# Unit 1's prefix products taken from the scan of all units, in a Mamba-2 SSD kernel with a SiLU MLP behind it

## The chip, the cores and the metric

The kernel runs on one core of one Trainium2 chip. The time is the device time of one execution in microseconds (us). A core has a matrix engine (PE), a vector engine (DVE), a scalar engine (ACT), GpSimd (POOL) and SyncE (SP), whose queue here issues most of the DMA transfers. Each engine runs its own instruction queue in order, and waits on semaphores for the others.

## The reference

Inputs are x (4, 8, 768, 32), a (4, 8, 768), B and C (4, 8, 768, 16) in single precision, and two weights, (256, 2048) and (2048, 256), in double precision. The first block is a chunked state-space scan, the second an MLP on its output.

```python
log_a = np.log(np.clip(a, 1e-06, 1.0))
for c in range(nc):                       # chunks along the sequence
    cum = np.cumsum(la, axis=-1)
    M = einsum('bhin,bhjn->bhij', Cc, Bc) * exp(cum_i - cum_j) * causal
    y = M @ xc + (Cc @ state) * exp(cum)[..., None]
    state = exp(sum(la)) * state + sum_j(B_j x_j * exp(cum[-1] - cum_j))
x = attn_out.transpose(0, 2, 1, 3).reshape(B * S, H * D)      # (3072, 256)
h = x @ w_in
return (h * (1 / (1 + exp(-h)))) @ w_out                      # (3072, 256)
```

## The kernel before

The sequence is cut into 12 **units** of 256 rows, three for each batch, and a unit into chunks of 64. A unit u goes through these steps; the names are those of the schedule's tokens.

- **Loads**: `Ln` (B or C with rows on partitions), `Lt` (B or C in a layout for a 32x32 transpose), `Lx` (x), `lw` (a weight tile of 512 KB, in the double's two words).
- **Prefix products** of a inside a chunk, which replace the exponential of a cumulative sum: a scan along the free axis that multiplies, and restarts at each chunk because a zero stands at its first place and a one is added there. They are kept in `PFX[u]`, spread over 16 partitions for each head.
- **E**: the decay between two positions, a scan (L512) over a diagonal. For units 0 and 1 its input is made on the chip (`ia`, `A`, `AT`, `AU`, `as`, `ab`: load, clip, transpose, copy, copies, four transposes on PE). For later units `La` loads it from a DRAM buffer `az`.
- **B** scales B by E's last column (POOL, L520). **T** transposes C and B on DVE (L525), **tp/tq** on PE and ACT. **ce** masks C for the even and odd heads (ACT, with `par`, which `cP` makes). **g0** is C times B (PE, L585), **M** multiplies it with E (DVE, L600). **D** or **gd** is B times x (PE, L571), **S** the running state (DVE, L615), **SM** its masked copy (ACT), **C** is C times the prefix (L551, DVE or POOL), and **Y** the unit's output on PE (L635, L644).
- **The MLP**: units 0 and 1 use single-precision matmuls (`s`, L697, first layer; `n1`, L761, second layer). Later pairs of units split numbers in three parts (`xh`, `x`, `h`, `l`, `e`) and use `a`, `d` (L800) and `q` (L782). Each weight tile is first turned from doubles into singles: `u`, `v` on ACT (L294, L297), `w` on DVE (L303, L307, L310), `W` on POOL (L318), and then split by `H`, `lD`, `dD` and others.
- **z** is a warm-up matmul on zeros (L441).

**Two ways to a prefix.** Units 0 and 1 have their own: `ip` loads the unit's 256 values of a for all heads, each repeated on 16 partitions (L379); `P01` clips them (L475) and scans (L479). All other units read theirs from a DRAM buffer `ac`: `ir` loads a as 48 chunks by 8 heads in four parts (L383); `AA` clips it on POOL (L462), once for `az` and once for the scan; `AP` scans all chunks of all units in one DVE instruction over 48 partitions by 520 (L486); `AD` stores the result, `AD,4` to `az` (L468) and `AD,0` to `AD,3` one batch each to `ac` (L470); `Lp,u` loads a unit's part of `ac`, spread over 16 partitions, on SP (L237). `ca` and `co` are the memsets for the zeros and ones of that scan.

**The order** is written out by hand in `SCHEDULE`, a string of tokens that are carried out one after the other: each engine's queue holds its instructions in the order of the tokens, and `SLOTS` names the buffer that each tile takes. In the old order the steps for `ac` come late: `ir` is spread over the places after unit 1's Y, `AP` ran at 39.5 us, and unit 1's own prefix stands between the transposes and the first MLP matmul:

```text
u,5 w,5,0 ip,1,0 z,1 P01,1,0 tp,1 tq,1 s,0,0 ce,1,1 ce,1,0 g0,1 Lx,1,1,0 Lx,1,0,0 W,4 xh,0 w,5,1 si,0,0 B,1,0 P01,1,1 D,1
```

Of the kernel before, what the change touches and what calls it, by code (L numbers as in the profile page):

```python
# [28 lines left out]
Wd,12 x,0,1 lw,14 u,14 n1,11,0 n1,9,1 x,1,1 W,8 Ln,2,1,0,0 v,14 w,14,2 ir,0 si,1,0 n1,1,0 n1,1,1 H,0 n1,0,1 H,1 lw,6 v,6
w,6,2 n1,11,1 n1,10,1 ir,2 ir,1 u,6 lw,10 Wl,12 AA,0 AA,1 AD,4 w,6,0 AP w,6,1 AD,0 lw,2 Ln,2,0,0,0 ax,0,7 w,15,0 u,10  # L30
u,2 W,6 n1,8,0 AD,1 v,2 H,6 v,10 w,2,0 s,1,1 si,1,1 lw,3 tp,2 dD,7 v,3 v,15 u,3 w,2,1 w,2,2 W,2,0 Lt,3,1,3,0 lD,6 dD,6
w,14,0 n1,8,1 w,3,2 a,0,6 ax,0,6 w,15,2 W,2,1 s,1,2 si,1,2 H,2 d,0,7 w,14,1 dg,0,7 AD,2 w,3,0 w,15,1 d,0,6 dg,0,6 W,14
Lt,3,1,0,0 w,10,2 s,0,2 lw,9 u,9 v,9 Lt,3,1,2,0 Lt,3,1,1,0 T,3,1 H,4 si,0,2 n1,10,0 Lx,2,0,0 n1,12,1 La,2,0,0 w,3,1 tq,2
La,2,1,0 E,2,1 E,2,0 lD,4 w,9,0 W,15 n1,15,1 Lt,3,0,0,0 n1,12,0 B,2 ce,2,0 ce,2,1 Lt,3,0,3,0 g0,2 lw,11 u,11 Lp,2,0 C,2
M,2,1 Lx,2,1,0 gd,2 b,2,0 b,2,1 S,2,0 S,2,1 H,15 S,2,2 W,3 Lp,3,0 Lt,4,1,1,0 H,13 La,3,1,0 w,10,0 v,11 Lt,4,1,0,0
n1,15,0 SM,2,0 Wl,15 SM,2,1 w,10,1 W,10 ce,3,1 Lt,4,1,3,0 M,2,0 La,3,0,0 E,3,1 E,3,0 s,0,3 si,0,3 Lt,3,0,2,0 ce,3,0
n1,13,0 Lt,3,0,1,0 T,3,0 Y,2 Lx,3,1,0 Ln,3,0,0,0 y,2,0 y,2,1 xh,2 x,2,0 n1,5,0 x,2,1 Ln,3,0,1,0 s,1,3 w,9,1 g0,3 C,3 B,3
M,3,1 Lx,3,0,0 gd,3 b,3,0 b,3,1 S,3,0 S,3,1 Lt,4,0,1,0 w,9,2 n1,0,0 n1,14,1 Lx,4,0,0 Lt,4,0,0,0 La,4,0,0 S,3,2 W,9
n1,13,1 SM,3,0 M,3,0 SM,3,1 lD,0 Y,3 n1,2,1 n1,3,0 Lt,4,0,3,0 dD,0 La,4,1,0 w,11,0 w,11,1 y,3,0 y,3,1 xh,3 x,3,0 w,11,2
n1,2,0 W,11 H,10 a,1,0 Wl,10 Wm,10 n1,3,1 n1,4,0 Lt,4,1,2,0 T,4,1 x,3,1 si,1,3 S,3,3 Lp,4,0 C,4 ce,4,1 E,4,0 H,11 ax,1,0  # L40
d,1,0 E,4,1 ce,4,0 Lt,4,0,2,0 n1,5,1 Wl,11 Lx,5,1,0 Wl,13 dg,1,0 n1,4,1 T,4,0 H,8 lD,1 Ln,4,0,0,0 g0,4 lD,2 Ln,4,0,1,0
B,4 H,9 M,4,1 La,5,1,0 Wm,11 Lx,4,1,0 Wm,12 gd,4 b,4,0 lD,8 b,4,1 dD,1 n1,6,1 h,1,0 S,4,0 S,4,1 Lx,5,0,0 H,3 S,4,2
SM,4,1 n1,14,0 n1,6,0 SM,4,0 Lt,5,1,3,0 M,4,0 n1,7,0 Vn,0 Y,4 y,4,1 y,4,0 xh,4 l,1,0 n1,7,1 S,4,3 a,1,2 Vn,1 lD,9 dD,8
dD,2 H,5 a,1,1 ax,1,2 e,1,0 q,1,0,1,0 d,1,2 dD,9 q,1,0,0,1 Ln,5,0,0,0 ax,1,1 d,1,1 Wd,13 Lt,5,1,1,0 q,1,0,0,0 q,1,0,1,1
AD,3 Lt,5,1,0,0 dD,4 dg,1,2 Lt,5,0,3,0 h,1,2 a,1,4 dg,1,1 h,1,1 Lt,5,1,2,0 T,5,1 ce,5,0 Lt,5,0,2,0 ce,5,1 Lt,5,0,0,0
lD,3 a,1,3 Lp,6,0 dD,10 o,0,1,2 We,12 dD,3 x,4,1 x,4,0 l,1,2 e,1,2 ax,1,4 d,1,4 H,14 q,1,2,0,1 Ln,5,0,1,0 ax,1,3 d,1,3
l,1,1 La,5,0,0 E,5,0 dg,1,4 e,1,1 q,1,1,1,1 dg,1,3 Lt,5,0,1,0 h,1,3 q,1,1,0,1 E,5,1 T,5,0 g0,5 B,5 M,5,1 Lp,5,0 C,5 gd,5
b,5,1 lD,5 Lt,6,1,0,0 b,5,0 S,5,0 Lt,6,1,3,0 S,5,1 Wm,13 We,13 dD,5 q,1,2,1,1 La,6,0,0 q,1,2,0,0 a,1,5 Lx,6,1,0 Wl,14
# [840 lines left out]
```

## Time and profile before

| | us |
|---|---|
| median of three runs | 329.66 |
| lowest, highest | 329.29, 333.11 |
| the profiled execution | 329.1 |
| its span from the first to the last instruction | 327.4 |
| PE busy | 320.3 (98%) |
| DVE busy | 240.4 (73%) |
| ACT busy | 209.5 (64%) |
| POOL busy | 56.0 (17%) |
| granted clock, mean | 0.999 |

A row of the profile names the line of the kernel, the engine, the operation, what it writes and reads by tile names, and sizes as partitions by elements. In the timelines a row begins with its start from the span's start and its duration, and ends with the idle time of its engine before it and what ended that. Durations of neighbours on one engine overlap by some hundredths, so that the distance between starts is a little shorter than the duration.

### The profile page before, as it was taken

To read this page: it belongs to the slowest core of one execution; us is meant where nothing else is said; L and a number is where in the kernel's file an instruction comes from. 1 tells how busy PE (TensorE), PEld (TensorE's weight loads), DVE (VectorE), ACT (ScalarE), POOL (GpSimd) and SP (SyncE) were. 2 spreads that over 40 slices of the span, in tenths; PEclk is the share of its full clock that TensorE was granted. 3 is DMA by queue.
4 is the path that set the end of the run, shared out by engine and by line. 5 is a ranking of instruction groups with operands and counts; after the bars stand their busy time and mean duration, and the time that the engine had idled before them with its cause. 6 is when DMAs were issued, how large, how long until landed. Compare 5 with 4: busy or idle time off the path is not lost.

```text
span 327.4 us, 7519 instructions
## 1 busy us (share of the span) xinstructions
PE 320.3 (98%) x3064; PEld 243.4 (74%) x3067; DVE 240.4 (73%) x331; ACT 209.5 (64%) x319; POOL 56.0 (17%) x74
## 2 busy tenths in 40 slices
PE   8999999999999999999999999999999999999994
PEld 3478576655687777878887778878887788888883
DVE  4998999999988965877687299665787544635553
ACT  4679978648696846583771875837775455574641
POOL 1364766326102330001200010010001000000000
PEclk9999999999999999999999999999999999999999
DMA  6979966479872663423633306514042000050003
GB/s 162 206 200 272 296 175 192 51 148 135 148 127 46 105 115 53 86 36 64 147 74 70 44 1 117 104 26 96 3 74 37 7 2 2 0 88 0 2 1 64
DMA packets 94962, 29.27 MB, mean 89 GB/s; under 512 B 80000, under 2 KB 86912, under 8 KB 94928
## 3 DMA queue, kind: packets, MB, share of 16 engines
q1 hardware_dynamic: 90960, 25.71, 37.5%
q0 software_dynamic: 1616, 2.82, 5.1%
q10 hardware_dynamic: 2352, 0.26, 0.6%
q8 instruction: 24, 0.39, 0.5%
q14 instruction: 10, 0.08, 0.1%
HBM read 22.81 MB, written 3.34 MB: 80 GB/s over the span
## 4 chain that ended last, share of the span: by engine, by line
PE 94%; SPq 2%; DMA 1%; DVE 1%; issue 1%; DVEq 0%
PE hp L782 29%; PE ga L800 18%; PE gb L800 18%; PE hp L761 9%; PE hp L697 6%; PE o_ps L782 6%; PE ga L635 2%; PE ga L585 2%; PE ga L644 2%; DMA s2k<-in_C_dram 1%; PE gb L644 1%; PE ga L571 1%; SPq L262 0%; SPq L375 0%; PE o_ps L531 0%
## 5 line engine op out<-in xcount | busy, mean ns | idle before, releaser
L782 PE MATMUL hp<-r4k,s2k 128*128 128x512 f32 x400 | 110.0, 394 | 0.0
L651 DVE SCALAR_TENSOR_TENSOR r4k<-r4k,r4k 128x1024 fp32r<-128x1024 f32 (+1 forms) x42 | 50.5, 1202 | 51.3 <-ACT r4k L827 48.2
L782 PEld LDWEIGHTS hp<-r4k,s2k 128*128 128x128 f32 x400 | 74.0, 188 | 16.4 <-issue 0.3
L800 PE MATMUL ga<-raw,s2k 128*128 128x512 f32 x240 | 62.3, 395 | 0.0
L800 PE MATMUL gb<-raw,s2k 128*128 128x512 f32 x240 | 61.1, 390 | 0.0
L800 PEld LDWEIGHTS ga<-raw,s2k 128*128 128x128 f32 x240 | 44.7, 188 | 11.4 <-ACT ga L811 0.9
L800 PEld LDWEIGHTS gb<-raw,s2k 128*128 128x128 f32 x240 | 44.8, 188 | 9.9 <-ACT gb L811 0.5
L837 DVE SCALAR_TENSOR_TENSOR r4k<-r4k,r4k 128x1024 fp32r<-128x1024 f32 x40 | 49.2, 1231 | 3.4 <-DVE r4k L651 0.9
L827 ACT ACTIVATE r4k<-r4k 128x1024 fp32r<-128x1024 f32 x40 | 42.2, 1058 | 3.2 <-issue 1.3
L811 ACT ACTIVATE ga<-ga 128x1024 f32<-128x1024 f32 x21 | 21.1, 1007 | 24.6 <-PE ga L800 23.8
L811 ACT ACTIVATE gb<-gb 128x1024 f32<-128x1024 f32 x21 | 21.2, 1009 | 17.6 <-PE gb L800 13.3
L782 PE MATMUL o_ps<-r4k,s2k 128*128 128x512 f32 x80 | 30.7, 390 | 0.0
L761 PE MATMUL hp<-r4k,s2k 128*128 128x512 f32 x64 | 30.0, 602 | 0.0
L821 ACT ACTIVATE r4k<-gb 128x1024 f32<-128x1024 f32 x21 | 21.4, 1021 | 12.4 <-PE gb L800 9.9
L520 POOL TENSOR_TENSOR BT<-bn,ab 128x256 f32<-128x256 f32 x10 | 6.7, 672 | 129.5 <-DVE ab L512 123.3
L318 POOL TENSOR_TENSOR s2k<-s2k,s2k 128x512 uint32<-128x512 uint32 (+1 forms) x19 | 23.6, 1250 | 26.4 <-DVE s2k L307 13.7
L821 ACT ACTIVATE r4k<-ga 128x1024 f32<-128x1024 f32 x21 | 21.5, 1023 | 8.4 <-PE ga L800 8.2
L512 DVE TENSOR_TENSOR_SCAN ab<-ab,diag 128x512 f32<-128x512 f32 x20 | 24.8, 1265 | 0.0
L697 PE MATMUL hp<-r4k,s2k 128*128 128x256 f32 x96 | 22.3, 382 | 0.2 <-issue 0.2
L697 PEld LDWEIGHTS hp<-r4k,s2k 128*128 128x128 f32 x96 | 18.0, 190 | 4.0 <-issue 1.4
L761 PEld LDWEIGHTS hp<-r4k,s2k 128*128 128x128 f32 x64 | 11.6, 189 | 10.5 <-issue 9.6
L782 PEld LDWEIGHTS o_ps<-r4k,s2k 128*128 128x128 f32 x80 | 15.0, 188 | 3.2
(123 smaller groups left out, 384.8 us busy)
## 6 DMA issues: line engine op xcount, KB each, us to landing
ab<-az SPq DMA_DIRECT2D x20, 256.0 KB, 4.2
raw<-in_moe_w_in_dram SPq DMA_DIRECT2D x8, 512.0 KB, 4.2
raw<-in_moe_w_out_dram SPq DMA_DIRECT2D x8, 512.0 KB, 8.0
...
xt<-in_x_dram SPq DMA_DIRECT2D x20, 128.0 KB, 4.2
...
```

Of the source, the lines that this page charges most:

```text
L318: nc.gpsimd.tensor_tensor(out=u[:, :, fs], in0=u[:, :, fs], in1=v[:, :, fs], op=ALU.add)
L512: nc.vector.tensor_tensor_scan(out=o, data0=src, data1=diag.rearrange("p h t -> p (h t)"), initial=0.0, op0=ALU.mult, op1=ALU.add)
L644: nc.tensor.matmul(out=y[w][32 * q:32 * q + 32, c, 64 * k:64 * k + 64], lhsT=xc[64 * c:64 * c + 64, k, h], rhs=m[64 * c:64 * c + 64, k, h] ...
L651: nc.vector.scalar_tensor_tensor(out=l, in0=f32(h), scalar=BACK, in1=y, op0=ALU.mult, op1=ALU.add)
L697: nc.tensor.matmul(out=hp[:, i], lhsT=WT[j][:, kc, 128 * i:128 * i + 128], rhs=XM()[:, 2 * kc:2 * kc + 2, u], start=(kc == 0), stop=(kc == ...
L761: nc.tensor.matmul(out=NP[m], lhsT=WT[8 + f // 2][:, f % 2, 128 * m:128 * m + 128], rhs=GT[0, f // 2][:, f % 2], start=(n == 1), stop=(n = ...
L782: nc.tensor.matmul(out=ACC[P, c], lhsT=WK[8 + i, p][:, k, 128 * m:128 * m + 128], rhs={"h": HT, "l": LT, "d": DT}[p][P, i][:, k], start=(n ...
L800: nc.tensor.matmul(out=o, lhsT=WK[j, q][:, kc, 128 * i:128 * i + 128], rhs=xs[:, 2 * kc:2 * kc + 2], start=(start and q == "h" and kc == 0 ...
L811: nc.scalar.activation(t, t, AF.Copy, scale=1.0 + Z)
L821: nc.scalar.activation(g, t, AF.Silu, scale=BACK)
L827: nc.scalar.activation(t, GT[G, i], AF.Copy, scale=-LESS * Z)
L837: nc.vector.scalar_tensor_tensor(out=DT[G, i], in0=f32(HT[G, i]), scalar=-1.0, in1=f32(LT[G, i]), op0=ALU.mult, op1=ALU.subtract)
```

## The change

Unit 1 no longer makes a prefix of its own. `ip,1`, `P01,1,0` and `P01,1,1` leave the schedule (one load, one clip and one scan, with a memset), and `Lp,1` comes in: unit 1 reads its part of `ac` as the later units do. The steps that fill `ac` for batch 0 (`ir`, `ca`, `AA`, `co`, `AP`, `AD,0`) move ahead of unit 0's first matmuls on x. All other tokens are the same in kind and number, among them all loads, matmuls and warm-up matmuls, and stand in a new order from the first to the last; the buffer lists are new to match.

```diff
     def c_p01():
-        for u in range(2):
-            nc.vector.memset(pz01(u)[:, :, 0:1], 0.0)
+        nc.vector.memset(pz01(0)[:, :, 0:1], 0.0)
         nc.vector.memset(one01(), 0.0)
         nc.vector.memset(one01()[:, :, 0:1], 1.0)
...
 SCHEDULE = """
-Ln,0,0,0,1 ia,1 ci z,1 z,1 z,1 z,1 z,1 z,1 ia,0 Ln,0,0,1,1 cI z,1 ch cP ct ip,0,0 z,1 z,1 z,1 c1 cd A AT cp AU lw,0 z,1
-z,1 as,0,0 ab,0,0 P01,0,0 P01,0,1 as,0,1 ab,0,1 as,1,1 ab,1,1 E,0,0 u,0 z,1 z,1 z,1 Lt,0,1,3,0 v,0 w,0,0 w,0,2 w,0,1
-lw,4 W,0,1 z,1 B,0,0 z,1 z,1 v,4 Lt,0,1,1,0 u,4 z,1 z,1 Ln,1,1,1,0 z,1 E,0,1 B,0,1 z,1 z,1 z,1 Lt,0,1,0,0 Lt,0,1,2,0
-T,0,1 as,1,0 z,1 z,1 z,1 tp,0 tq,0 E,1,1 Lx,0,0,0 Lx,0,1,0 D,0 S,0,0 z,1 w,4,2 z,1 S,0,1 z,1 w,4,0 S,0,2 ce,0,0 ce,0,1
-g0,0 M,0,1 lw,7 v,7 Ln,1,0,0,0 SM,0,0 M,0,0 z,1 z,1 SM,0,1 u,7 w,4,1 w,7,0 z,1 z,1 w,7,2 w,7,1 lw,5 v,5 w,5,2 W,0,0
-S,0,3 Ln,1,1,0,0 ab,1,0 E,1,0 C,0 Y,0 X0,0,1 Ln,1,0,1,0 B,1,1 X0,0,0 u,5 w,5,0 ip,1,0 z,1 P01,1,0 tp,1 tq,1 s,0,0 ce,1,1
-ce,1,0 g0,1 Lx,1,1,0 Lx,1,0,0 W,4 xh,0 w,5,1 si,0,0 B,1,0 P01,1,1 D,1 s,0,4 M,1,1 lw,1 u,1 lw,12 S,1,0 W,5 v,1 ca S,1,1
...
+Ln,0,0,1,1 cI ci z,1 ch z,1 z,1 z,1 z,1 z,1 z,1 c1 z,1 Ln,0,0,0,1 cd ia,1 ir,0 z,1 ct z,1 ia,0 A z,1 Lt,0,1,0,0 AT AU
+as,0,1 Lx,0,1,0 as,0,0 z,1 cp ir,2 ip,0,0 P01,0,0 P01,0,1 z,1 ab,0,1 E,0,1 as,1,1 ab,1,1 tp,0 tq,0 ca ir,1 ab,0,0 z,1
+z,1 ir,3 AA,0 E,0,0 lw,4 Lt,0,1,3,0 u,4 B,0,1 z,1 z,1 Lt,0,1,1,0 z,1 z,1 Lt,0,1,2,0 T,0,1 cP z,1 ce,0,1 z,1 z,1 v,4 AA,1
+co AP z,1 ce,0,0 z,1 w,4,0 E,1,1 w,4,2 lw,0 z,1 z,1 z,1 Ln,1,0,1,0 z,1 Lx,0,0,0 z,1 AD,0 B,0,0 g0,0 M,0,1 Ln,1,0,0,0 z,1
+D,0 as,1,0 S,0,0 S,0,1 z,1 u,0 v,0 w,0,0 z,1 S,0,2 SM,0,1 M,0,0 w,0,1 w,0,2 ab,1,0 z,1 E,1,0 B,1,1 z,1 Ln,1,1,0,0 lw,5
+SM,0,0 u,5 S,0,3 w,5,0 C,0 v,5 w,4,1 Y,0 X0,0,0 X0,0,1 xh,0 z,1 Ln,1,1,1,0 tp,1 ce,1,1 W,0,0 w,5,2 W,0,1 s,0,0 lw,7
+ce,1,0 Lp,1,0 tq,1 C,1 B,1,0 w,5,1 g0,1 M,1,1 Lx,1,1,0 Lx,1,0,0 D,1 S,1,0 u,7 si,0,0 S,1,1 S,1,2 lw,1 SM,1,1 v,1 u,1
+lw,8 SM,1,0 W,4 w,7,0 S,1,3 s,0,4 M,1,0 Lt,3,1,1,0 w,1,2 v,7 v,8 W,5 s,0,5 w,1,0 w,1,1 W,1,1 u,8 w,8,0 w,7,2 si,0,5 lw,6
...
```

Three new helper functions (`w_copy`, `f_ds`, `f_dl`) are defined, and no token of the schedule calls them.

More of the change, by code (lines that the diff above doesn't have):

```diff
@@ L29 @@
[L29 to L48, printed above, removed]
@@ new lines @@
+lD,4 Ln,5,0,1,0 n1,5,0 n1,3,1 M,4,0 n1,7,0 Vn,0 Y,4 y,4,1 l,1,0 n1,2,1 lD,8 lD,2 dD,2 y,4,0 La,5,0,0 lD,9 dD,8
+Lt,5,1,3,0 xh,4 dD,5 Lt,5,1,1,0 Lt,5,1,2,0 T,5,1 e,1,0 dD,1 Wl,15 Wm,15 Lt,5,0,3,0 a,1,2 ax,1,2 Vn,1 o,0,1,2 ce,5,1
+Lt,5,0,0,0 a,1,1 ax,1,1 d,1,2 dg,1,2 q,1,0,1,0 Lt,5,0,1,0 dD,9 q,1,0,0,0 Wd,15 h,1,2 x,4,1 Wd,12 O,0,1,2,1,0 d,1,1
+Lt,5,0,2,0 AD,3 We,13 ce,5,0 q,1,0,1,1 dg,1,1 h,1,1 q,1,0,0,1 Wm,12 dD,4 S,4,3 a,1,4 ax,1,4 a,1,3 l,1,2 e,1,2 dD,10
+q,1,2,1,1 Lx,5,0,0 ax,1,3 La,5,1,0 d,1,4 dg,1,4 Lp,5,0 d,1,3 dg,1,3 h,1,3 q,1,2,0,1 l,1,1 e,1,1 q,1,1,1,0 E,5,0 E,5,1
@@ L100 @@
+O,5,0,2,2,0 Va,5,1 qd,5,7,0,1 qd,5,6,0,1 qd,5,7,1,1 Vt,5,1,0 Vt,5,1,1 ot,5,1,0 Vt,5,1,3 Vt,5,1,2 ot,5,1,1 or,5,1,0
+os,5,1,0,0 or,5,1,1 os,5,1,1,1
 """
@@ L335, in w_part, with w_copy @@
         nc.scalar.activation(t, f32(WK[n, "h"]), AF.Copy, scale=1.0 if p == "l" else Z)
+    def w_copy(n):
+        t = WK[n, "l"] = small(f"l{n}", [128, 2, WF], FR)
+        nc.sync.dma_start(out=f32(t).rearrange("p k f -> p (k f)"), in_=f32(WK[n, "h"]).rearrange("p k f -> p (k f)"))
     def w_more(n, p):
@@ L755, with f_ds, f_dl @@
     NP = {}
+    def f_ds(i):
+        spill[i] = dram.tile([128, 1024], FP32, name=f"spill{i}")
+        nc.sync.dma_start(out=spill[i], in_=GT[0, i].rearrange("p k n -> p (k n)"))
+    def f_dl(i):
+        g = GT[0, i] = large(f"R0_{i}", [128, 2, 512])
+        nc.sync.dma_start(out=g.rearrange("p k n -> p (k n)"), in_=spill[i])
+    spill = {}
     def f_n(f, m):
```

136 lines of the change are left out of this document (74 added, 62 removed), and 6 rows, old and new, of the table SLOTS.

## The prediction

> **What bounds the kernel now.** I read the page's first part and its stage table first, since they say which engine is full and where it is not.
>
> ```profile
> span 327.4 us, 7519 instructions
> PE 320.3 (98%) x3064; PEld 243.4 (74%) x3067; DVE 240.4 (73%) x331; ACT 209.5 (64%) x319; POOL 56.0 (17%) x74
> ...
> 0.00:10.00 10.00, 8.45 (x34) 3.95 (x35) 5.71 (x21) 3.78 (x6) 1.41 (x10) 1.00 0.73 163
> 10.00:20.00 10.00, 9.21 (x191) 5.87 (x199) 9.57 (x19) 7.95 (x19) 5.18 (x8) 1.00 0.88 185
> 20.00:30.00 10.00, 9.72 (x193) 8.15 (x193) 8.76 (x20) 7.54 (x16) 5.49 (x9) 1.00 0.97 289
> 30.00:40.00 10.00, 10.00 (x37) 6.62 (x36) 9.52 (x12) 9.16 (x17) 6.84 (x7) 1.00 0.90 264
> ```
>
> The columns of a stage are its length, then busy time of PE, PEld, DVE, ACT and POOL, then the granted clock, the DMA share and GB/s. From 30 us on to the tail PE is busy for all of every stage, so the time is set by when PE's dense stretch begins, by PE's own work after that, and by the tail. The change cannot shorten PE's work (its list has the same matmuls, the 36 warm-up ones included), so I look for the step that opens the dense stretch, in the chain of waits and in PE's timeline:
>
> ```profile
> 6.36 4.75 DMA s2k<-in_C_dram
> 14.38 1.21 DVE ab L600 x2
> 15.73 0.27 PE ga L635 x2
> ...
> 1.27 4.45 PE L441 MATMUL o_ps<-s2k 128*128 128x512 bf16 x10 [1.27 <-DVE s2k L388]
> 8.07 3.40 PE L441 MATMUL o_ps<-s2k 128*128 128x512 bf16 x15
> 17.25 0.83 PE L531 MATMUL o_ps<-ident,s2k 128*128 128x128 f32 x4 [0.16 <-issue]
> 17.94 1.99 PE L697 MATMUL hp<-r4k,s2k 128*128 128x256 f32 x8
> ```
>
> Unit 0's output Y (L635) starts at 15.73, when VectorE (DVE) has finished M (L600); its transposes (L531) and then the first MLP matmul (L697, at 17.94) follow. Before 17.94 PE mostly runs warm-up matmuls. The last long wait on that path is the C load, landing at 11.11; after it DVE works without a break.
>
> **The head, step by step.** In the new order unit 0's head has more ahead of it, and I walk the two queues that matter. These are DVE's and ACT's rows; a cost below is the distance from one start to the next where DVE runs without a break.
>
> ```profile
> 2.32 0.22 DVE L422 TENSOR_REDUCE par<-hm 128x1 f32<-128x4 f32 x2 [0.97 <-POOL hm L417]
> 4.10 0.22 DVE L448 TENSOR_SCALAR s2k<-s2k 32x128 f32<-32x128 f32 x1 [0.41 <-DMA s2k<-in_a_dram]
> 4.46 0.28 DVE L410 MEMSET s2k<- 128x260 f32 x1
> 6.22 0.43 DVE L495 COPY s2k<-s2k 128x512 f32<-128x512 f32 x1
> 6.56 0.29 DVE L475 TENSOR_SCALAR s2k<-s2k 128x256 f32<-128x256 f32 x1
> 6.88 0.70 DVE L479 TENSOR_TENSOR_SCAN s2k<-s2k,s2k 128x260 f32<-128x260 f32 x1
> 7.50 1.20 DVE L512 TENSOR_TENSOR_SCAN ab<-hp,diag 128x512 f32<-128x512 f32 x1
> 8.61 0.40 DVE L303 TENSOR_SCALAR s2k<-s2k 128x512 f32<-128x512 f32 x1
> 8.93 0.69 DVE L310 SCALAR_TENSOR_TENSOR s2k<-raw,s2k 128x512 uint32<-128x512 uint32 x1
> ...
> 11.30 0.65 DVE L525 STREAM_TRANSPOSE ct<-s2k 128x256 f32<-128x256 f32 x1 [0.21 <-DMA s2k<-in_C_dram]
> 11.79 1.17 DVE L512 TENSOR_TENSOR_SCAN ab<-hp,diag 128x512 f32<-128x512 f32 x1
> ...
> 14.11 0.28 DVE L615 SCALAR_TENSOR_TENSOR st<-st,s2k,hp 128x64 f32<-128x64 f32 x1
> 14.30 0.69 DVE L600 TENSOR_TENSOR ab<-gb,ab 128x512 f32<-128x512 f32 x1
> ...
> 36.99 1.09 DVE L310 SCALAR_TENSOR_TENSOR s2k<-raw,s2k 128x512 uint32<-128x512 uint32 x1
> 39.51 1.23 DVE L486 TENSOR_TENSOR_SCAN r4k<-r4k,r4k 48x520 f32<-48x520 f32 x1
> ```
>
> And the loads and GpSimd (POOL) steps, as SP's and POOL's timelines and the list of DMA issues show them:
>
> ```profile
> 0.81 1.64 SPq L375 DMA_DIRECT2D s2k<-in_a_dram  x2
> 2.50 0.63 SPq L379 DMA_DIRECT2D s2k<-in_a_dram  x1
> 20.73 0.45 SPq L383 DMA_DIRECT2D s2k<-in_a_dram  x1
> ...
> 10.04 0.73 POOL L318 TENSOR_TENSOR s2k<-s2k,s2k 128x256 uint32<-128x256 uint32 x1 [6.81 <-DVE s2k L307]
> 10.73 0.85 POOL L520 TENSOR_TENSOR BT<-s2k,ab 128x128 f32<-128x128 f32 x2
> 26.63 0.52 POOL L425 MEMSET r4k<- 48x520 f32 x1
> 36.61 0.93 POOL L462 TENSOR_SCALAR s2k<-s2k 48x512 f32<-48x512 f32 x1
> 37.78 0.77 POOL L462 TENSOR_SCALAR r4k<-s2k 48x512 f32<-48x512 f32 x1
> 41.05 0.63 POOL L470 DMA_DIRECT2D ac<-r4k  x1 [1.68 <-DVE s2k L307]
> ...
> xt<-in_x_dram SPq DMA_DIRECT2D x20, 128.0 KB, 4.2
> ac<-r4k POOLq DMA_DIRECT2D x4, 24.4 KB, 4.0
> az<-s2k POOLq DMA_DIRECT2D x1, 96.0 KB, 6.0
> ```
>
> *SP.* One of the four chunk loads (ir, L383, 0.45 us of SP each) now stands between the two ia loads, so the second ia is issued 0.5 us later and the clip (4.10) comes at 4.6. That costs nothing by itself: the transpose of a (AT) stands behind warm-up matmuls on PE, 11 of them instead of 10, at 0.445 us each, so it starts near 6.2 instead of 5.7, and the copies after it 0.45 us later. The load ip for unit 0's prefix is now seventh on SP: 0.81 + 1.64 for the ia pair, two ir, a C load and an x load at about 0.45 each, with gaps of 0.05, gives an issue at 4.5 instead of 2.50. Before, its user (L475) ran at 6.56 without a wait for it, so it landed within 4.06 us of its issue; the ia load took 2.35 (issued at 1.75, used at 4.10). So it lands between 6.85 and 8.55, and I take the middle, 7.7.
>
> *DVE up to the first scan.* The copy (6.67), its 0.34 and the three memsets (about 0.45 together, moved behind it) end at 7.45. The prefix then waits for ip: 7.7 + 0.32 + 0.62 puts the scan E (L512) at 8.64 instead of 7.50; bounds 8.4 and 9.5.
>
> *DVE from that scan to M.* Now in the list: two scans 2.22, the C transpose 0.49, two reductions for par 0.22, the scan of all units (L486) 1.15, one weight clip 0.32, a third scan 1.11, one weight merge 0.60, M's first half 0.60, two state steps 0.38, another clip 0.32, a state step 0.19, and M's second half 0.69: 8.29 us. The C loads are not late for it: their last is issued as the 13th on SP, near 7.5, and lands at the older spacing by 11, when the two scans end. The scan of all units waits for POOL: B of unit 0 (0.42, behind the first scan, 9.8), clip 0.77, the memsets of ones 0.52 + 0.10, ready at 11.7 where DVE arrives at 11.57: 0.15 of wait. The POOL clips and memsets now run beside this chain; the merge at 36.99 took 1.09 instead of 0.69 beside such a clip, so I add 0.4 (bounds: 0, and 1.0 if two or three instructions stretch). End of M: 8.64 + 8.29 + 0.15 + 0.4 = 17.5, and Y starts 0.1 behind it, as before, at 17.6 instead of 15.73.
>
> *Unit 0's x and weight 0.* The second half of x is issued 16th. Ahead of it stand the same transfers as before and four ir loads of 24 KB: 0.5 us at the 185 GB/s of that stage, 1.8 by their issue time. Even 1.8 would land it near 14.5, with D right behind, and D's first user on DVE only runs at 16.2. Weight 0 is cleaned right behind M (0.32 + 0.60) and added on POOL in two halves (L318, 0.73 each): ready at 19.9. PE needs 2.21 from Y to the first MLP matmul, plus one warm-up matmul (0.23) that now stands ahead of the transposes: 17.6 + 2.21 + 0.23 = 20.05, against 17.94. **Shift of the dense stretch: +2.1 us** (bounds +1.4 and +3.6, from the two ends of the first scan's start and of the stretch).
>
> **Unit 1's own prefix goes, a wait comes.** Its load, clip and scan leave (clip and scan about 1.0 of DVE, by unit 0's rows). PE is not waiting for DVE there, so this pays nothing directly. In their place: the store of the scan of all units (L470) right after that scan ends at 13.0 (11.7 + 1.23), landed 4.0 later, at 17.0; then Lp,1 on SP, then unit 1's prefix. Behind the waiting Lp,1 in SP's queue stand both x loads of unit 1, then weights 1 and 8. The prefix is issued at 17.0 and, at the 4.2 of the other loads (xt), lands at 21.2; DVE comes to its user C,1 near 21.2 (seven instructions behind M, one of them a scan). The last x load is issued at 18.5 and lands at 22.7; PE wants it for D,1 behind the first L697 group (1.9) and G (0.8 by my estimate), at 22.75. So the cover is just used up: I put +0.1 us, 0 if the store lands earlier; the upper bound is the first rival.
>
> **The rest.** From Y of unit 1 on both lists hold the same work and PE's row is full before. I added the row durations in list order, and asked at each PE instruction how far its producer's queue is ahead of PE's. For DVE the smallest lead between 10 and 70 us of PE work is 4.6 before and 4.8 after; for ACT the lead at unit 4's Y falls from 2.4 to 0.9. These are estimates from durations alone, so I put 0 for the middle, with 1.5 as the upper bound. The tail keeps three d-matmuls behind the last copy and four stores ahead of the last two; two more half-groups of matmuls behind the first copy are 0.1 us at most.
>
> **Sum.** The profiled execution took 329.1 us around its span of 327.4: 329.1 + 2.1 + 0.1 + 0.1 = **331.4 us**, 0.5% over the median of the runs shown (329.66), of which the profiled one lies 0.6 below. About 2% (6.6 us) is what a measurement of this kernel tells from no change, so the forecast is no change, on the slow side; its own range is 330.3 to 333.0.
>
> **Rivals.**
> - *The store gates SP (slower).* If the store lands as late as az did (6.0 instead of 4.0), Lp,1 is issued at 19.0, unit 1's x lands at 24.7 and D,1 waits 2.0: 333.3. Each us later costs one more, and the weights queued behind come later too; a store landing at 22.1, 9 us after its issue, crosses the 2%. It speaks for this that the DMA share is 0.88 to 0.97 in these stages; against, that the store is 24 KB and az 96 KB. It decides from a landing later than 17.0.
> - *The head hardly moves.* If ip lands by 6.85, the early warm-up matmuls speed up sooner (0.227 instead of 0.445 each, so AT is not held), and nothing stretches beside POOL, the first scan starts at 7.8 (6.85 + 0.94) and M ends at 16.2: a shift of 0.8 instead of 2.1 and no wait at D,1, 330.0; the runs of before reach down to 0.4 us under the median, so this would be read as no change at all. For it: only such small steps hold DVE up; against: the scan of all units and the third scan stay ahead of M.
> - *ACT falls behind in the middle:* the lost lead of 1.5 us at unit 4's Y turns into a PE wait, 332.9. For it: ACT is busy 9.16 of 10 us in one stage; against: DVE's and POOL's leads hold.
> - *PE slows again in the head.* Between D and Y PE has only 4 warm-up matmuls and four transposes for some 3 us (7 warm-up matmuls before). Its first ten took 0.445 each, later ones 0.227, though the clock column says 1.00 in both. If it falls back to the slower pace for as long as at the start (4.45 us), half of that, 2.2 us, is lost: 333.6.
>
> The Trainium skill (TensorE: Matmul & The Clock Gate, Part 1: The HAM clock gate) says the array runs at half rate until a window of about 3.4 us has been busy, and falls back after an idle one; by that rule the last rival's slowdown would come true only if a whole window went idle. The trace agrees with the half rate at the start (0.445 against 0.227); no run so far shows a fall back.
>
> **How the numbers follow.** Forecast 45%, store gating SP 20%, head hardly moving 20%, ACT behind 10%, PE slow again 5%. The range 329.0 to 335.4 reaches over the second rival at its lower end and over most of the first at its upper one, and leaves out some 15%. Faster by over 2% would need 6.6 us where all of PE's idle time in the span is 7.1: 1%. Slower by over 2%: a quarter of the first rival, and mixes of several: 7%. Within: 92%.
>
> **What would show it.** Right: L600's second M ends near 17.4, the first L697 starts near 20.0, L571 of unit 1 with no wait or a short one, PE full after that. Wrong: L697 before 18.5 (DVE's chain is shorter than I walked), a PE wait of over 1 us at L571 (the store), or PE gaps after 40 us.

## The result and the profile after

The changed kernel takes 332.81 us (median of 20 executions, 332.49 to 335.72) against 329.56 for the kernel before (328.47 to 333.11): a ratio of 1.0096 with a 95% interval of 1.0081 to 1.0112. It is 3.2 us slower, about 1%. That is less than the 2% that was set as the bound for a difference, but the interval leaves out a ratio of 1. The forecast was 331.4.

The profiled execution took 332.82 (329.1 before). The first part of its page and its stages, in the columns explained above:

```profile
span 331.1 us, 7508 instructions
PE 322.1 (97%) x3067; PEld 242.7 (73%) x3067; DVE 235.0 (71%) x328; ACT 209.9 (63%) x319; POOL 55.2 (17%) x74
...
0.00:10.00 10.00, 8.20 (x32) 3.73 (x33) 4.15 (x14) 3.02 (x5) 2.19 (x13) 1.00 0.54 122
10.00:20.00 10.00, 7.92 (x181) 4.66 (x180) 9.61 (x20) 6.36 (x14) 5.21 (x10) 1.00 0.95 215
20.00:30.00 10.00, 9.70 (x193) 7.46 (x192) 8.75 (x19) 7.66 (x17) 5.74 (x8) 1.00 1.06 307
30.00:40.00 10.00, 10.00 (x42) 7.69 (x41) 6.63 (x14) 7.95 (x15) 4.61 (x3) 1.00 0.98 250
```

PE lost its time between 10 and 20 us, where it is busy 7.92 instead of 9.21. From 30 us on it is as full as before, and the granted clock stays at 1.00. The timelines of the head of after follow (the lines of the kernel are three to thirteen higher than before: L638 was L635, L700 was L697, L515 was L512, L489 was L486).

```profile
17.92 0.27 PE L638 MATMUL ga<-cw,sm 32*64 32x64 f32 x2 [1.09 <-ACT sm L626]
19.88 1.89 PE L700 MATMUL hp<-r4k,s2k 128*128 128x256 f32 x8
26.56 0.27 PE L638 MATMUL ga<-cw,sm 32*64 32x64 f32 x2
28.60 5.66 PE L700 MATMUL hp<-r4k,s2k 128*128 128x256 f32 x25 [0.23 <-POOL s2k L318]
...
8.00 0.29 DVE L478 TENSOR_SCALAR s2k<-s2k 128x256 f32<-128x256 f32 x1 [0.36 <-DMA s2k<-in_a_dram]
8.95 2.31 DVE L515 TENSOR_TENSOR_SCAN ab<-hp,diag 128x512 f32<-128x512 f32 x2
12.08 1.23 DVE L489 TENSOR_TENSOR_SCAN r4k<-r4k,r4k 48x520 f32<-48x520 f32 x1 [0.27 <-POOL r4k L429]
17.07 0.68 DVE L603 TENSOR_TENSOR ab<-ga,ab 128x512 f32<-128x512 f32 x1
21.59 0.42 DVE L554 TENSOR_TENSOR cw<-o_ps,pfx 128x256 f32<-128x256 f32 x1
...
13.63 0.82 POOL L473 DMA_DIRECT2D ac<-r4k  x1 [1.58 <-DVE r4k L489]
...
17.44 0.62 SPq L237 DMA_DIRECT2D pfx<-ac  x1
18.11 1.25 SPq L269 DMA_DIRECT2D s2k<-in_x_dram  x2
```

The chain is the one that was walked: the load for unit 0's prefix ends a wait of 0.36 at 8.00, the first scan E starts at 8.95, the scan of all units stands in the middle of DVE's row at 12.08, M's second part ends at 17.75, unit 0's Y starts at 17.92 and the first MLP matmul at 19.88. Unit 1's prefix load (L237) is issued at 17.44, and its user on DVE (L554, at 21.59) has no wait mark: by the trace the last part of the load landed at 20.68, 0.9 us before.

The same places before, and the tails. The first two lines are before's PE timeline at unit 1's Y and at the third group of MLP matmuls; the rest is its tail, then the tail of after.

```profile
24.77 0.27 PE L635 MATMUL ga<-cw,sm 32*64 32x64 f32 x2
26.41 7.07 PE L697 MATMUL hp<-r4k,s2k 128*128 128x256 f32 x32 [0.16 <-issue]
...
321.14 1.07 PE L782 MATMUL o_ps<-r4k,s2k 128*128 128x512 f32 x4
321.62 1.94 SPq L719 DMA_DIRECT2D out_dram<-r4k  x4
323.74 0.39 SPq L750 DMA_DIRECT2D out_dram<-s2k  x1
324.08 0.39 ACTq L750 DMA_DIRECT2D out_dram<-s2k  x1
```

```profile
324.56 0.84 PE L795 MATMUL o_ps<-r4k,s2k 128*128 128x512 f32 x3
325.04 2.27 SPq L722 DMA_DIRECT2D out_dram<-r4k  x4
327.41 0.43 SPq L753 DMA_DIRECT2D out_dram<-s2k  x1
```

From these rows the 3.7 us between the spans (331.1 − 327.4) divide as follows:

| stretch | before | after | difference |
|---|---|---|---|
| span start to the first MLP matmul | 17.94 | 19.88 | +1.94 |
| from there to the third group of them | 8.47 | 8.72 | +0.25 |
| the dense stretch, from there to the end of the last output matmul | 295.80 | 296.80 | +1.00 |
| the tail, from there to the end of the span | 5.19 | 5.70 | +0.51 |

So the head carries half of the loss; the other half comes at places that the forecast put at nearly nothing.

### The profile page after: what moved, and what is told of

It is laid out like the page before. It is cut to its first block, busy times and chain, and to the rows that moved or that the text cites. A ratio compares the mean times of both kernels' runs of the same rounds, so it can differ in the third digit from the quotient of the medians.

```text
span 331.1 us, 7508 instructions
## 1 busy us (share of the span) xinstructions
PE 322.1 (97%) x3067; PEld 242.7 (73%) x3067; DVE 235.0 (71%) x328; ACT 209.9 (63%) x319; POOL 55.2 (17%) x74
## 4 chain that ended last, share of the span: by engine, by line
PE 91%; DVE 4%; SPq 1%; DMA 1%; ACT 1%; POOL 0%; issue 0%; DVEq 0%
PE hp L795 28%; PE ga L813 18%; PE gb L813 17%; PE hp L774 9%; PE o_ps L795 6%; PE hp L700 5%; PE ga L588 2%; PE ga L638 2%; PE ga L647 2%; PE ga L574 1%; PE gb L647 1%; DMA s2k<-in_a_dram 1%; DVE ab L515 1%; DVE ab L603 1%; SPq L379 0%; POOL s2k L318 0%
## 5 line engine op out<-in xcount | busy, mean ns | idle before, releaser
L795 PE MATMUL hp<-r4k,s2k 128*128 128x512 f32 x400 | 111.8, 394 | 0.0
L824 ACT ACTIVATE ga<-ga 128x1024 f32<-128x1024 f32 x21 | 21.2, 1008 | 22.7 <-PE ga L813 18.3
L824 ACT ACTIVATE gb<-gb 128x1024 f32<-128x1024 f32 x21 | 21.2, 1008 | 22.7 <-PE gb L813 22.7
L523 POOL TENSOR_TENSOR BT<-bn,ab 128x256 f32<-128x256 f32 x10 | 7.7, 767 | 139.0 <-DVE ab L515 67.2
L774 PE MATMUL hp<-r4k,s2k 128*128 128x512 f32 x64 | 30.2, 602 | 0.0
L515 DVE TENSOR_TENSOR_SCAN ab<-ab,diag 128x512 f32<-128x512 f32 x20 | 24.0, 1215 | 0.0
L700 PE MATMUL hp<-r4k,s2k 128*128 128x256 f32 x96 | 22.1, 382 | 0.2 <-POOL s2k L318 0.2
L700 PEld LDWEIGHTS hp<-r4k,s2k 128*128 128x128 f32 x96 | 17.9, 190 | 4.4 <-issue 1.2
```

The source lines that it names most:

```text
L515: nc.vector.tensor_tensor_scan(out=o, data0=src, data1=diag.rearrange("p h t -> p (h t)"), initial=0.0, op0=ALU.mult, op1=ALU.add)
L700: nc.tensor.matmul(out=hp[:, i], lhsT=WT[j][:, kc, 128 * i:128 * i + 128], rhs=XM()[:, 2 * kc:2 * kc + 2, u], start=(kc == 0), stop=(kc == ...
L774: nc.tensor.matmul(out=NP[m], lhsT=WT[8 + f // 2][:, f % 2, 128 * m:128 * m + 128], rhs=GT[0, f // 2][:, f % 2], start=(n == 1), stop=(n = ...
L795: nc.tensor.matmul(out=ACC[P, c], lhsT=WK[8 + i, p][:, k, 128 * m:128 * m + 128], rhs={"h": HT, "l": LT, "d": DT}[p][P, i][:, k], start=(n ...
L824: nc.scalar.activation(t, t, AF.Copy, scale=1.0 + Z)
```

## The experiments

Besides the cause that was predicted (theory H: the longer row of DVE ahead of unit 0's Y) three rivals were to be told apart: that the store and the load through DRAM gate unit 1 (G), that the new order costs the time and the change itself does not (O), and that the end is slower for its own reasons (T). The expectations call H theory A, G theory B and O theory C (T is "theory C for the tail"); `s,0,1` in a schedule is the first token of the third group of MLP matmuls. A ratio is to the kernel before on the same chip in the same set of runs.

**own_prefix.** After, with unit 1's own prefix put back and the rest of the order kept.

```diff
+ip,1,0                 (ahead of Ln,1,1,0,0)
+P01,1,0 P01,1,1        (ahead of ce,1,0)
-Lp,1,0
```

> Edit: after's order, but unit 1 takes its prefix products from its own bound and scan again (load of 256 values, one bound, one scan on VectorE ahead of unit 1's read-out product), so nothing waits on SP for the store of the scan of all units; the scan of all units, its loads and its store stay in the head. Theory A (VectorE's longer chain ahead of unit 0's decay products delays PE's dense start): the first L700 stays at 19.9 us, time within 0.3 us of after (332.5 to 333.1). Theory B (the load of the prefix products blocks SP's queue for 3 us and what stands behind it comes late): PE's wait for L318 at 28.6 us goes, time 0.3 to 0.6 us under after (332.2 to 332.5). Theory C (the new order as such costs): as after, 332.8.

It took 334.31, a ratio of 1.014 (1.0105 to 1.0174), so 1.0 us more than after in the profiled executions and 1.5 in the medians. Its first MLP matmul starts where that of after does (19.88), with unit 0's Y at 17.56 instead of 17.92. PE's, DVE's and POOL's timelines between there and unit 1's Y:

```profile
25.82 1.97 PE L700 MATMUL hp<-r4k,s2k 128*128 128x256 f32 x8 [1.09 <-DVE st L618]
27.71 0.27 PE L638 MATMUL ga<-cw,sm 32*64 32x64 f32 x2
...
21.19 1.37 DVE L478 TENSOR_SCALAR s2k<-s2k 128x256 f32<-128x256 f32 x1
22.59 0.70 DVE L482 TENSOR_TENSOR_SCAN pfx<-s2k,s2k 128x260 f32<-128x260 f32 x1
...
20.74 1.66 POOL L318 TENSOR_TENSOR s2k<-s2k,s2k 128x512 uint32<-128x512 uint32 x1 [0.36 <-DVE s2k L307]
```

The own clip and scan hold DVE for 2.07 us. The state steps (L618) come 1.15 later than in after (24.70 against 23.55), and the matmuls that need the PSUM buffer they free wait 1.09. Y of unit 1 comes 1.15 later than in after, too. So in this order the step that leaves does pay, and G has the opposite sign: the load through DRAM is better than the unit's own prefix.

**own_scan_late.** The same, and the scan of all units with its memsets, clips and stores moved behind unit 1's Y.

```diff
-ca AA,0 ... AA,1 co AP ... AD,0     (in unit 0's head)
+ca AA,0 AA,1 co AP AD,0             (ahead of AD,4, behind Y,1)
```

> Edit: as the run with unit 1's own prefix, and the two bounds on POOL, the scan of all units on VectorE and its first store on POOL move from the head to behind unit 1's output matmuls; the four loads of a stay in the head. Theory A: the first L700 starts 1.3 to 1.6 us earlier (18.3 to 18.6 us), since the scan (1.15) and its wait (0.27) leave VectorE's chain, and the time is 331.2 to 331.5. Theory B: as the run with unit 1's own prefix and no less. Theory C: the start of L700 and the time stay as in after (332.8).

It took 336.33, a ratio of 1.0188 (1.0152 to 1.0225). PE's and ACT's timelines and one stage:

```profile
16.98 0.27 PE L638 MATMUL ga<-cw,sm 32*64 32x64 f32 x2 [0.57 <-ACT sm L626]
20.28 0.66 ACT L294 ACTIVATE s2k<-raw 128x512 f32<-128x512 f32 x1 [3.40 <-DMA raw<-in_moe_w_in_dram]
...
20.00:25.00 5.00, 3.47 (x8) 2.66 (x9) 3.86 (x7) 3.95 (x9) 1.64 (x1) 0.58 0.81 210
```

Unit 0's Y comes 0.94 earlier than in after (17.92) and 0.58 earlier than in own_prefix (17.56), from which this run differs by the scan alone. Five executions with the same head (after, after_again, own_prefix, old_tail, x_first) have this Y between 17.56 and 18.04, so the scan's share of the head is 0.6 to 0.9. But the load of weight 5 is issued at 14.54 instead of 12.72, with the own load ahead of it in SP's queue, and lands at 20.26 instead of 16.91 (why it took so long is not shown). ACT waits 3.40 us for it with the copies of unit 0's output queued behind, PE runs dry, and the granted clock falls to 0.58. The time is thus no measure of the scan; only Y's start is.

**own_loads_late.** The same, and the four loads of a (`ir`) moved behind unit 1's x loads as well.

```diff
-ir,0 ... ir,2 ... ir,1 ... ir,3     (in unit 0's head)
+ir,0 ir,1 ir,2 ir,3                 (behind Lx,1,0,0)
```

> Edit: as the run with the scan moved behind unit 1, and the four loads of a move behind unit 1's loads of x, too. Theory A: unit 0's own bound no longer waits 0.36 us for its load, the first L700 starts another 0.2 to 0.4 us earlier (18.0 to 18.3 us), time 330.8 to 331.2; what is then left over the kernel before is the new order (dense stretch +1.0, tail +0.5). Theory B: as the run before it. Theory C: 332.8, no earlier start.

It took 333.53, a ratio of 1.0113 (1.0082 to 1.0144). PE's timeline, and DVE's row for unit 1's own clip:

```profile
15.65 0.27 PE L638 MATMUL ga<-cw,sm 32*64 32x64 f32 x2 [0.59 <-ACT sm L626]
17.87 1.97 PE L700 MATMUL hp<-r4k,s2k 128*128 128x256 f32 x8
26.58 0.27 PE L638 MATMUL ga<-cw,sm 32*64 32x64 f32 x2 [0.72 <-ACT sm L626]
...
19.27 1.36 DVE L478 TENSOR_SCALAR s2k<-s2k 128x256 f32<-128x256 f32 x1
```

The head is that of before again: Y at 15.65 (15.73 before), the first MLP matmul at 17.87 (17.94). So H holds for the head: without the scan's steps and loads its 2 us are gone, of them 0.6 to 0.9 with the scan and 1.33 more (16.98 to 15.65) with the four loads on SP. Yet unit 1's Y comes at 26.58, where after has it at 26.56: the own prefix gives all of it back. The rest, up to a time 0.7 over after's, comes later. The four loads, late now, hold SP for 4.96 us from 16.07 on, with a weight's load behind them, and PE waits 0.7 (at 28.75) and 0.9 (at 38.6) for POOL's sums of weights.

**old_order.** The change in the order of before: `Lp,1` for `ip,1` and `P01,1`, and the steps for `ac` set among before's tokens.

```diff
-ip,1,0 ... P01,1,0 ... P01,1,1
+ir,0 (behind ia,1)  ir,1 ir,2 ir,3 (around ip,0,0)  ca (behind cp)
+AA,0 (behind B,0,0)  AA,1 co (behind B,0,1)  AP (behind T,0,1)
+AD,0 (ahead of tp,0)  Lp,1,0 (ahead of Lx,1,1,0)
```

> Edit: the kernel before with the change alone and its own order: the four loads of a, the bounds, the scan of all units and its first store in the head (scan behind unit 0's transpose of C on VectorE, store on POOL behind unit 0's B products), unit 1's prefix products read back ahead of its loads of x, unit 1's own load, bound and scan gone. Theory A: PE's first matmul of the expert layer starts 1.2 to 1.6 us later than in before (17.9), the rest is as in before, time 330.7 to 331.2. Theory B: the same start as before, a wait at unit 1 (0.3 to 0.6), time 329.9 to 330.2. Theory C: all of the loss belongs to the new order, so 329.4 to 329.8 here.

It took 335.4, a ratio of 1.0167 (1.0133 to 1.0201). DVE's and PE's timelines:

```profile
15.02 1.23 DVE L486 TENSOR_TENSOR_SCAN r4k<-r4k,r4k 48x520 f32<-48x520 f32 x1 [1.63 <-POOL r4k L426]
20.61 0.37 PE L635 MATMUL ga<-cw,sm 32*64 32x64 f32 x2 [2.54 <-ACT s2k L294]
```

The scan waits 1.63 for the memset of ones, which stands on POOL behind a weight sum, Y comes 4.9 later than before, and the clock falls to 0.66 from 20 to 25 us. This placing of the change in the old order is not free; a better one stays open here, since what is late is a memset on POOL, which stands behind a weight sum, two products B and both clips. From the third MLP group on this run is before's again (295.72 to the last output matmul, tail 5.1).

**order_alone.** The new order with unit 1's own prefix, its load in the place of `Lp,1`, and the steps for `ac` late.

```diff
-Lp,1,0
+ip,1,0 (its place)  P01,1,0 P01,1,1 (ahead of C,1)
+ir x4 (behind lw,2)  ca AA,0 AA,1 co AP AD,0 AD,4 (behind W,6)
```

> Edit: after's order without the change. The four loads of a, the two bounds, the scan of all units and both stores move behind unit 1, among the first second-product matmuls; unit 1 has its own load (in the place where the load of its prefix products stood on SP), bound and scan (ahead of its read-out product on VectorE). Theory A (the added VectorE steps ahead of unit 0's and unit 1's decay products delay PE): the first L700 at 17.9 to 18.3 us instead of 19.9, s,0,1 at 27.4 to 28.0 instead of 28.9, time 331.2 to 331.8; what is left over the kernel before is the order's own (dense stretch +1.0, tail +0.5). Theory B (the block on SP): the same start of L700 as in after, gain 0.3. Theory C (the new order carries the loss): 332.5 to 333.

It took 338.46, a ratio of 1.0256 (1.0225 to 1.0287). PE's timeline at unit 1's Y, and POOL's after it:

```profile
26.43 0.27 PE L638 MATMUL ga<-cw,sm 32*64 32x64 f32 x2
...
44.17 6.08 POOL L318 TENSOR_TENSOR s2k<-s2k,s2k 128x512 uint32<-128x512 uint32 x3
```

Up to unit 1's Y it is within 0.13 of after (26.43 against 26.56), though its first MLP matmul starts 1.6 earlier, at 18.26. Then the late steps stand on POOL ahead of three weight sums that PE needs (PE is busy 5.87 of the 10 us from 40 on). So the time says nothing of the order; the rows to 26.43 say that in the new order the change is nearly even at unit 1's Y: the head pays 1.6, the own prefix that leaves gives it back. They say one thing more: with the own prefix and the late scan the new order reaches unit 1's Y at 26.43 (26.58 in own_loads_late), 1.7 to 1.8 behind the 24.77 of before, and so as late as after.

**scan_cut.** After, with the scan of all units over 65 of its 520 columns (the rest of its products is left out).

```diff
-    ... [:, 0:520]
+    ... [:, 0:65]        (in f_AP, line 489)
```

> Edit: after with the scan of all units run over 65 of its 520 elements (the rest of the prefix products is left out); no instruction is added, removed or moved. Theory A: the scan takes 0.2 to 0.3 instead of 1.23 us, the first L700 and s,0,1 come 0.8 to 1.0 us earlier, time 331.8 to 332.1. If PE's start is held by something else than VectorE's chain (ScalarE's ce, the store's late pieces), less than 0.3 us moves. Theory B: 332.8, or 332.5 with the store issued 0.9 earlier. Theory C: 332.8.

It took 334.09, a ratio of 1.0123 (1.0097 to 1.0149): slower than after with less work. DVE's, ACT's and PE's timelines:

```profile
11.97 0.29 DVE L489 TENSOR_TENSOR_SCAN r4k<-r4k,r4k 48x65 f32<-48x65 f32 x1 [0.28 <-POOL r4k L429]
18.03 0.70 ACT L294 ACTIVATE s2k<-raw 128x512 f32<-128x512 f32 x1 [0.57 <-DMA raw<-in_moe_w_in_dram]
19.71 1.97 PE L700 MATMUL hp<-r4k,s2k 128*128 128x256 f32 x8
23.65 0.26 PE L588 MATMUL ga<-ce,bh 32*64 32x128 f32 x1 [1.62 <-issue]
30.05 0.32 PE L647 MATMUL gb<-ab,s2k 64*32 64x64 f32 x13 [0.78 <-issue]
```

The scan is 0.94 shorter, and the first MLP matmul gains 0.17. Behind DVE's chain a second one is due at the same place: the load of weight 5, which ACT turns into singles (L294) in front of the copies of unit 0's output. That shortening one of the two pays nothing is what this run suggests, not more: Y came 0.36 earlier (17.56), DVE waited 0.30 for POOL on the way and one clip took 0.87 instead of 0.44, and weight 5 landed at 18.01, where after has it at 16.91 and after_again at 18.04. The 2.4 us lost later are two stalls of PE without any semaphore; they are told of at the end.

**x_first.** After, with the loads of unit 1's x ahead of `Lp,1` on SP.

```diff
-Lp,1,0 ... Lx,1,1,0 Lx,1,0,0
+Lx,1,1,0 Lx,1,0,0 Lp,1,0
```

> Edit: after with unit 1's two loads of x ahead of the load of the prefix products on SP, so that only the weight loads behind it still wait for the store. Theory A: nothing on VectorE moves, time within 0.2 of after (332.6 to 333.0), the loads of x issued at 14.5 instead of 18.1 us. Theory B: the blocked x loads and the later weight loads cost 0.3 to 0.6, so 332.2 to 332.5, and PE's wait for the sum of w,1 (0.23) goes.

It took 334.68, a ratio of 1.0147 (1.0122 to 1.0172); in the profiled executions it is 0.6 over after. SP's and DVE's timelines:

```profile
18.12 1.19 SPq L237 DMA_DIRECT2D pfx<-ac  x1
22.25 0.42 DVE L554 TENSOR_TENSOR cw<-o_ps,pfx 128x256 f32<-128x256 f32 x1 [0.52 <-ACT s2k L294]
```

The loads of x gain nothing by going first, and the prefix load issued 0.7 later costs 0.5 at unit 1's Y (27.04). So x was not late behind the waiting `Lp,1`. The prefix load held SP for 1.19 instead of 0.62 here and landed at 22.13, 1.45 later than in after, which is where the wait of 0.52 ends (the row names ACT). In after the prefix has 0.9 us to spare, in after_again 0.55 and in scan_cut 0.23. Rival G falls for the kernel as it is, with little to spare.

**old_tail.** After, with the last tokens in the order of before.

```diff
+q,5,3,0,1 (ahead of Va,5,1)
+Vt,5,1,1 Vt,5,1,0 ot,5,1,0 or,5,1,0 os,5,1,0,0 Vt,5,1,2 Vt,5,1,3 ot,5,1,1 or,5,1,1 os,5,1,1,1   (the end)
```

> Edit: after with the last steps in the order of the kernel before: three more matmuls stand behind the last step of the first output half, the last four VectorE additions and the two transposes alternate as before, the first row store is issued ahead of the second half's work. Theory C for the tail: the end comes 5.2 instead of 5.7 us after the last matmul into o_ps, time 332.2 to 332.4. If the tail's length is set by the last stores' own landing alone, 332.8.

It took 333.19, a ratio of 1.0101 (1.0078 to 1.0123): not told apart from after. PE's and SP's timelines at the end:

```profile
324.19 1.07 PE L795 MATMUL o_ps<-r4k,s2k 128*128 128x512 f32 x4
324.90 2.29 SPq L722 DMA_DIRECT2D out_dram<-r4k  x4
```

The tail is 5.54 (330.8 − 325.26) where after has 5.70 and before 5.19. The order of the last tokens explains 0.16 of the 0.51 at most. The four stores on SP take 2.27 in after and 2.29 here, and 1.94 in the profile before, and SP's last store stands behind them; T comes up again below.

**after_again.** After with its buffers named by use, otherwise the same program.

> After as it is (the buffers are named by use instead of by position, the program is the same), beside the runs of this set. All theories: 332.5 to 333.2. If the runs so far stand higher because of the chip they ran on and not because of their edits, this one stands higher, too (333.5 to 334.5).

It took 332.66, a ratio of 1.0095 (1.008 to 1.0111), its profiled execution 332.77 with the same span of 331.1. Its first MLP matmul started 0.45 later (20.33), its dense stretch took 296.45 against 296.80, and the end did not move. Two executions of one program thus differ by 0.45 in the head and by 0.35 in the dense stretch.

**old_placed.** The change in before's order again, with the four loads of a on ACT's queue and the scan's steps later.

```diff
+ir x4 on nc.scalar (behind ct)  co AA,1 (ahead of W,0,1)
+AP (ahead of E,1,1)  w,4,2 w,4,0 (behind M,0,0)
+AD,0 (behind C,0)  Lp,1,0 (behind Lx,1,0,0)
```

> Edit: the change in the order of the kernel before, placed so that it stands in nobody's way: the four loads of a on ScalarE's queue instead of SP's (they are issued while ScalarE has nothing to do), the bound on POOL ahead of the first weight sum, the scan on VectorE ahead of unit 1's first decay scan, two steps of weight 4 (1.1 us) moved behind unit 0's decay products to make room for it, the store behind unit 0's read-out product on POOL, the load of unit 1's prefix products behind unit 1's loads of x. Theory A in its strict form (what counts is the length of VectorE's in-order chain ahead of unit 0's and of unit 1's decay products; it is 0.1 longer ahead of the first, and as long as before ahead of the second): first L697 at 17.9 to 18.3 us, time 329.3 to 330.2. Theory C (the loss is the new order's): the same, 329.3 to 330. Theory B (whatever waits for a store and a load through memory loses): VectorE waits for the prefix products at unit 1's first state (21.8 us) by 0.5 to 1.5, time 330.3 to 331.

It took 335.84, a ratio of 1.0183 (1.0161 to 1.0206). One row of ACT's queue says why:

```profile
3.39 7.62 ACTq L383 DMA_DIRECT2D s2k<-in_a_dram  x3
```

Three issues held ACT for 7.62 us, so the copies for unit 0's scan began only at 11.05. This run says nothing of the change but where its loads must not stand.

**m_first.** After, with the third scan E and two weight steps moved behind M, to bring Y forward.

```diff
-E,1,1 w,4,0 w,4,2 (ahead of M,0,1)
+w,4,0 E,1,1 w,4,2 (behind w,0,2)   B,0,0 (ahead of AP)   u,5 w,5,0 v,5 (behind xh,0)
```

> Edit: after with unit 0's decay products freed of what stands ahead of them: two steps of weight 4 and unit 1's first decay scan behind them on VectorE, unit 0's first B product ahead of the store on POOL, the two magnitude steps of weight 5 behind the copies of unit 0's outputs on ScalarE. The sum of VectorE's work ahead of unit 1's decay products is unchanged. If the start of PE's first expert matmul decides (theory A as the prediction had it): the first L700 at 18.0 to 18.6 us, time 331.2 to 331.8. If VectorE's whole chain up to unit 1's decay products decides: the first L700 earlier by the same 1.5 us, s,0,1 at 28.5 to 29, time 332.4 to 333. Theory C: as the latter.

It took 336.67, a ratio of 1.0216 (1.0202 to 1.0229). The longest of PE's waits (total, count, longest) and one stage:

```profile
PE hp L505 <- DVE ab L515: 3.8, 1, 3.8
...
20.00:25.00 5.00, 4.67 (x100) 3.58 (x99) 2.09 (x4) 2.10 (x5) 3.63 (x5) 0.58 1.05 281
```

The transposes of unit 1 (L505) stand in PE's queue ahead of unit 0's Y and need the PSUM buffer that the moved scan frees: PE waits 3.8 us, and over the stage shown the clock is at 0.58. The third scan ahead of M is not idle ballast; it lets PE go on.

**old_pool.** The change in before's order, with the loads of a on POOL's queue.

```diff
+ir x4 on nc.gpsimd, ca co (behind c1)   AA,1 (behind B,0,1)   AP (behind S,0,0)
+w,4,2 w,4,0 w,4,1 (behind M,0,0)   ab,1,0 E,1,0 (ahead of w,7,0)
+AD,0 (behind C,0)   M,1,0 (behind M,1,1)   Lp,1,0 (behind lw,1)
```

> Edit: the change once more in the order of the kernel before, with what held up the two earlier placements taken away: the four loads of a on POOL's own queue (POOL has nothing to do between 3.2 and 10 us), the bound on POOL behind unit 0's B products, the scan on VectorE ahead of unit 0's second state in the place of two steps of weight 4, which stand behind unit 0's decay products, the store behind unit 0's read-out product, the load of the prefix products on SP behind the load of weight 1, unit 1's second decay product ahead of its states. VectorE's chain ahead of unit 0's and unit 1's decay products is as long as before. If the loss of after lies in where things stand in the queues and not in the scan, the store and the load themselves: the first L697 at 17.9 to 18.3 us, s,0,1 at 26.5 to 27.3, time 329.3 to 330.3. If a prefix read back through memory costs whatever its place: VectorE's or SP's wait for the store shows ahead of unit 1's states, s,0,1 at 28 or later, time 331 or more.

It took 332.16, a ratio of 1.0062 (1.0038 to 1.0086): the best placing found, and still 2.3 over before. DVE's and PE's timelines:

```profile
12.31 0.65 DVE L525 STREAM_TRANSPOSE ct<-s2k 128x256 f32<-128x256 f32 x1 [1.27 <-DMA s2k<-in_C_dram]
17.06 0.27 PE L635 MATMUL ga<-cw,sm 32*64 32x64 f32 x2 [0.93 <-ACT s2k L294]
```

Off SP's queue the four loads still cost: C, on which unit 0 waits, lands about 1 us later (the transpose waited 0.21 before), and Y comes 1.33 later. No version beat the kernel before.

## Where the prediction was right and where it was wrong

**The head: right, in size and place.** The shift of the first MLP matmul was put at 2.1 and is 1.94. Along the row: first scan E 8.64 forecast and 8.95 measured, ready time of the scan of all units 11.7 and 12.08, end of M 17.5 and 17.75, Y 17.6 and 17.92, first MLP matmul 20.05 and 19.88. Y came 0.32 later than forecast, 0.31 of it up to E already, and the leg from Y to the first MLP matmul, put at 2.44, took 1.96. That these two nearly cancel is luck: in after_again the same leg is 2.58. The stretch of 0.4 beside POOL hardly shows in the merge (0.78 where 0.69 is usual). What the walk did not see is the second chain over weight 5's load and ACT that is due at the same time (scan_cut). The four loads, counted as 0.45 us of issue each, are worth 1.3 us of the head together, more than the scan itself (0.6 to 0.9), as own_scan_late and own_loads_late show.

**The wait that comes: right.** The prefix load was put at 17.0 and goes out at 17.44, and no wait shows at its user or at D of unit 1. It was to land at 21.2, just when its user comes; it landed at 20.68, with its user at 21.59. So the cover is nearly used up, and a landing 1.45 later cost 0.5 (x_first). The rival by which the store gates SP did not come true.

**"This pays nothing directly": true of the order before only.** There PE was not waiting for DVE at unit 1's clip and scan. In the new order the two stand ahead of state steps that free a PSUM buffer for PE, and they cost 1.0 (profile) to 1.5 us (medians) in own_prefix. The sum does not suffer by it, since it walks the new order without the two: to credit them would have put the forecast lower still. But as a price of the step that leaves, nothing is too low in the order that the change comes with.

**The middle: mis-sized, 0 forecast and +1.0 measured.** The waits view of after shows no wait of PE's matmuls of more than 0.5 us behind 30 us, so the rival about ACT did not come as it was told, as one wait at unit 4's Y. Where the 1.0 went shows in the starts of PE's matmuls in eleven traces, from the third MLP group to the last output matmul. The usual step of each kind of MLP matmul times its count is 266.7 us in each run, and what is spent around changes of kind and in the small matmuls is 28.2 to 28.3 in all. Left are matmuls that take longer than their kind's usual step although nothing changes around them: 0.25 to 0.51 us together in the four runs in the old order (before, old_order, old_placed, old_pool), 1.03 to 1.51 in the seven in the new one. They are 0.05 to 0.14 us each and stand at the same places of PE's list in the four runs of the new order that were compared place by place (in after at 118.8, 124.5, 217.6, 223.0, 223.4 and 229.0 us, for example).

For about half of this the traces show a cause: the weight load at the start of such a group of matmuls waits, at all but one of these places for ACT, whose reading of the accumulator (ga or gb) ended 0.04 to 0.1 us earlier, so it starts late, and the matmul behind it takes longer. The pages show it for gb, in the idle time ahead of the weight loads: 0.5 us of it ended by ACT in before (first row) and 1.3 in after.

```profile
L800 PEld LDWEIGHTS gb<-raw,s2k 128*128 128x128 f32 x240 | 44.8, 188 | 9.9 <-ACT gb L811 0.5
L813 PEld LDWEIGHTS gb<-raw,s2k 128*128 128x128 f32 x240 | 44.5, 188 | 10.5 <-ACT gb L824 1.3
```

Each of the four runs in the old order has four such places, 0.26 us together; each of the seven in the new one has eight, 0.79 to 0.86. So some 0.55 of the 1.0 us is lead that ACT lost, as the rival had it, but in small pieces spread over the middle. Durations added up did not show it. The other 0.45 is tied to nothing here; two executions of one program differ by 0.35 in this stretch.

**The tail: mis-sized, 0.1 forecast and +0.5 measured.** The reason given (two more half-groups behind the first copy) was not it: with before's last tokens 0.16 came back in one profile and nothing in the medians. All runs in the old order have 5.0 to 5.2, those in the new one 5.3 to 5.9. In every trace the span ends 3.4 to 3.9 us after SP issues its last store, so what moves that store moves the end. It is issued 1.53 to 1.54 us after the last output matmul ends in the four runs in the old order, and 1.7 to 2.2 in the ten in the new one: 1.53 in before and 2.01 in after, 0.48 of the 0.51. In after it follows straight on the four row stores (327.41, behind an end at 327.31). These begin 0.23 later than in before, measured from the end of the last matmul, and hold SP for 2.27 instead of 1.94. Why they hold it longer stays open; three runs in the new order (own_loads_late, m_first, order_alone) have 1.94 or 1.95.

**The total: inside the range, in part by luck.** The spans were to differ by 2.3 and differ by 3.7. The head gave 0.16 less than its term; the other three stretches gave 1.76 where the sum had 0.2 for them. The forecast's own range, 330.3 to 333.0, had 1.5 for the middle as its bound, and holds 332.81 with 0.2 to spare.

**"PE slows again":** not in after, whose clock stays at 1.00, but in own_scan_late, old_order, m_first, old_placed and order_alone, where PE ran dry or thin for some microseconds.

**Is it the change or the order?** Three placings in the old order cost 2.3 to 6.4 us, each for a place of its own (POOL's queue, ACT's queue, the landing of C), so no run shows the change free there. In the new order the change is about even at unit 1's Y: without it, Y comes at 26.4 to 26.6, as late as with it and 1.7 to 1.8 behind before. So the scan's 2 us are shown for the first MLP matmul, and that the change itself makes the kernel slower than before is not shown. The 1.5 us of the middle and the tail go with the new order. A clean split would need a run of the new order alone that places the late steps without blocking POOL; there is none.
